# Value product in two portions a tile, early scores in more PSUM banks, sums of one element in an attention and mixer kernel

## The chip, the cores and the metric

The kernel runs on one core of a Trainium2 chip. The metric is the device time of one execution in microseconds (us). A core has five engines that work side by side, each through its own instructions in order: TensorE (PE, matrix products; its weight loads are listed as PEld), VectorE (DVE), ScalarE (ACT), GpSimd (POOL) and SyncE (SP), which here only issues DMA transfers. They meet at semaphores. Matrix products land in PSUM, eight banks of 2 KB per partition; DVE and ACT carry results from there to SBUF.

## The reference

Talking-heads attention, 4 batches (b), 12 heads, 448 positions, 64 elements a head, followed by an MLP mixer, all float32:

```
scores = einsum('bhij,hg->bgij', scale * q @ k.T, w_pre)     # heads mixed before the softmax
e      = exp(scores - max(scores))
attn   = e / (sum(e) + 1e-9)
attn   = einsum('bhij,hg->bgij', attn, w_post)               # heads mixed after it
x      = attn @ v                                            # then (B, 448, 768)
u      = x + (relu(x.T @ w_tok1) @ w_tok2).T
out    = u + relu(u @ w_ch1) @ w_ch2
```

## The kernel before

The first half of the time is attention, the second half the mixer, which the change does not touch.

**Tiles and groups.** The 448 query positions of a batch are cut into tiles of 120, 120, 120 and 88 rows (`IT`), so there are 16 tiles T. For each tile `qk` makes the scores S of all 12 heads, one pair of heads a call: two products into two PSUM banks, then two copies to SBUF. `regroup` rearranges S by DMA on SP: a group G is ten query rows of all 12 heads. A tile of 120 rows has 12 groups, one of 88 rows has 9 (eight of ten rows and one of eight). There are 180 groups. `first[T]` is the first group of tile T.

**Steps.** The groups are taken in steps of two (the last group of an 88-row tile is a step of its own; a group of eight rows goes through smaller matrices, `kpre8`, `kpost8`). For one step `pre` (L210) mixes the heads of both groups into a PSUM tile "pre" of two banks, `mx` (L220, DVE) takes the row maximum, `ex` (L228, ACT) the exponential with its row sum, `rec` (L237, L238 on DVE, L241 on POOL) adds 1e-9 to the sums of both groups in one instruction, takes the reciprocal, and scales the matrix `wr` that mixes the heads afterwards. Then for each group `post` (L253, PE) mixes the heads and transposes into a bank "post", and `hi` (L270, ACT) copies that bank to AT, the attention of the tile. `av` (L278, PE) multiplies one pair of heads of a finished tile with V into one bank "av"; a copy on DVE (L284) and a DMA on SP (L287) follow. The two heads of a pair go to the two halves of the columns of the PE array, `qk` of the later tiles and `post` use all columns.

**Order.** The order of instructions on every engine is that of the program text (a manual schedule). The main loop goes over the steps. In step i it issues the regroupings of later groups, then at the first group `pre` of step i+2, `rec` of step i+1, `mx` and `ex` of step i+2; then for each group `post`, `hi`, the value products due there, the scores due there, and conversions. What is due at which group stands in two tables, `qk_at` and `do`, filled ahead of the loop (L464 to L488): while the groups of tile U are worked on, `qk` makes the scores of tile U+2 and `av` the value product of tile U-1. Before, the six `av` of a tile are spread evenly, one at every second group of a 12-group tile.

**Conversions.** Scores of tiles 2 to 15 use operands split in two parts of a rounded type. `conv_k` (L126 on ACT, then L127 on POOL) and `conv_q` (L153, L154) make them. Tiles 0 and 1 use the raw K and Q (L180), with the copy of S on ACT for the first head of a pair and on DVE for the second; later tiles have both copies on DVE (L186).

**PSUM.** The eight banks are two "pre" tiles of two banks, two "post" banks and two "av" banks. A `qk` takes either both "av" banks or one "pre" tile.

**The start.** WARM products on zeros come first. Then `qk` of tile 0 (pairs in turn in "pre" and "av"), the first regroupings, and part of tile 1's `qk`; the rest of tile 1 comes inside the first two groups.

**The end of attention.** At the last tile's second group the pools for the mixer are opened (`open_prep`) and weight conversions (`cv_tick`) begin to share ACT, DVE and POOL; behind the last group come transposes `tr` and the `av` of tile 15.

Of the kernel before, what the change touches and what calls it, by code (L numbers as in the profile page):

```python
# [8 lines left out]
F32 = mybir.dt.float32  # L9
# [16 lines left out]
HP = H // 2  # L26
# [11 lines left out]
def attn_mixer_kernel(  # L38
# [12 lines left out]
    nc = tc.nc  # L51
# [12 lines left out]
    def en(name, **kw):  # L64
        p = tc.alloc_tile_pool(name=name, reuse_waits="tile", **kw)
        opens[name] = p
        return p
# [5 lines left out]
    ps_av = en("ps_av", bufs=2, space=PSUM)  # L73
# [4 lines left out]
    ps = en("ps", bufs=2, space=PSUM)  # L78
# [15 lines left out]
    for b in range(B):  # L94
        for t in range(4):
            n = IT[t][1]
# [67 lines left out]
            nc.sync.dma_start(out=V[b][p:p + n, :, part, :], in_=v[b, j % 128:j % 128 + n, :, j // 128, :])  # L164
            j += n

    def qk(T, h, split=False):
        b, t = divmod(T, 4)
        n = IT[t][1]
        if T not in S_t:  # L170
            S_t[T] = early.tile([120, H, S], F32, tag="s", name="s")
        if split:
            p2 = ps.tile([128, 2, 512], F32, tag="pre", name="qk")
            p = [p2[:, s] for s in range(2)]
        else:
            p = [ps_av.tile([128, 512], F32, tag="av", name="qk") for s in range(2)]
        for s in range(2):
            if T < 2:
                g, rs = HP * s + h, slice(64 * s, 64 * s + 64)
                nc.tensor.matmul(out=p[s][:n, :S], lhsT=Q[T][rs, h, :], rhs=K0[rs, h, :], start=True, stop=True)  # L180
            else:
                g = 2 * h + s
                kt = K[b, h][:, s, :]
                for i, l in enumerate(Q[T, g // 6]):
                    nc.tensor.matmul(out=p[s][:n, :S], lhsT=l[:, g % 6, :], rhs=kt, start=i == 0, stop=i == 1)  # L185
            (nc.vector.tensor_copy if s or T > 1 else nc.scalar.copy)(out=S_t[T][:n, g, :], in_=p[s][:n, :S])  # L186
# [9 lines left out]
    def regroup(G):  # L196
        b, t, c, n = groups[G]
        o = 4 if n == GR else 0
        nc.sync.dma_start(out=rt[G % NR][o:o + 12 * n], in_=rows(G)(S_t[4 * b + t], 0))

    def pre(st):
        p = ps.tile([128, 2, 512], F32, tag="pre", name="pre")
        PP[st[0]] = p
        if len(st) == 1:
            nc.tensor.matmul(out=p[:96, 0, :S], lhsT=kpre8, rhs=rt[st[0] % NR][:96], start=True, stop=True)
            return
        for x in range(2):
            k = slice(64 * x, 64 + 60 * x)
            for s, a in enumerate(st):
                nc.tensor.matmul(  # L210
                    out=p[64 * s:64 * s + 64, x, :S], lhsT=kpre[k], rhs=rt[a % NR][k], start=True, stop=True
                )

    def parts(G):
        return 128 if groups[G][3] == GR else 96
# [7 lines left out]
    def ex(st):  # L223
        m = parts(st[0])
        s, p = SM[st[0]], PP.pop(st[0])
        for x, G in enumerate(st):
            e = mid.tile([128, S], F32, tag="e", bufs=6, name="e")
            nc.scalar.activation(  # L228
                out=e[:m], in_=p[:m, x, :S], func=ACTF.Exp, bias=s[:m, x:x + 1], scale=1.0,
                accum_out=s[:m, 2 + x:3 + x],  # L230
            )
            E[G] = e

    def rec(st):
        m, w, n = parts(st[0]), len(st), groups[st[0]][3]
        s = SM.pop(st[0])
        nc.vector.tensor_scalar_add(out=s[:m, 4:4 + w], in0=s[:m, 2:2 + w], scalar1=1e-9)  # L237
        nc.vector.reciprocal(out=s[:m, 6:6 + w], in_=s[:m, 4:4 + w])  # L238
        for x, G in enumerate(st):
            r = mid.tile([128, 120], F32, tag="wr", bufs=4, name="wr")  # L240
            nc.gpsimd.tensor_scalar(  # L241
                out=r[:m, :12 * n], in0=kpost if n == GR else kpost8, scalar1=s[:m, 6 + x:7 + x], scalar2=None,
                op0=ALU.mult,
            )
            WR[G] = r
# [10 lines left out]
    def hi(G):  # L256
        b, t, c, n = groups[G]
        T = 4 * b + t
        if T not in AT:
            AT[T] = atp.tile([JP, JT, H, 120], F32, tag="at", bufs=2, name="at")  # L260
        d = AT[T].rearrange("p j g i -> p (j g) i")
        p = PO.pop(G)[:JP, :JT * H * n]
        if n < GR:
            d, p = d[:, :, 10:88:11], p.rearrange("p (q i) -> p q i", i=n)
        else:
            w = 10 if t < 3 else 11
            a = w * (c - c % 2)
            d = d[:, :, a:a + 2 * w].rearrange("p q (s i) -> p q s i", s=2)[:, :, :, 5 * (c % 2):5 * (c % 2) + 5]
            p = p.rearrange("p (q s i) -> p q s i", s=2, i=5)
        nc.scalar.copy(out=d, in_=p)  # L270
# [32 lines left out]
    for i in range(WARM):  # L303
        p = ps.tile([128, 512], F32, tag="post", name="pw")
# [3 lines left out]
    for x in range(2):  # L308
        ps_ = slice(64 * x, 64 * x + 64)
        nc.vector.tensor_tensor(  # L310
            out=kpre[ps_, :60].rearrange("p (i g) -> p i g", i=5),
            in0=kcat[0][ps_, :12].unsqueeze(1).to_broadcast([64, 5, H]),
# [4 lines left out]
        out=kpost.rearrange("p (g i) -> p g i", g=H), in0=kcat[1][:, 12:24].unsqueeze(2).to_broadcast([128, H, GR]),  # L317
# [5 lines left out]
        out=kpre8.rearrange("p (i g) -> p i g", i=8), in0=k8[:, :12].unsqueeze(1).to_broadcast([96, 8, H]),  # L323
# [4 lines left out]
        out=kpost8.rearrange("p (g i) -> p g i", g=H), in0=k8[:, 12:24].unsqueeze(2).to_broadcast([96, H, 8]),  # L328
        in1=k8[:, 24:32].unsqueeze(1).to_broadcast([96, H, 8]), op=ALU.mult,
    )  # L330
    for h in range(HP):
        qk(0, h, h % 2 == 0)
    for G in range(NR):
        regroup(G)
    for h in range(2):
        qk(1, h)
    steps = []
    G = 0
    while G < NG:
        n = 2 if groups[G][2] % 2 == 0 and groups[G][3] == GR else 1  # L340
# [2 lines left out]
    pre(steps[0])  # L343
    mx(steps[0])
    ex(steps[0])
    pre(steps[1])
    qk(1, 2)
    rec(steps[0])
    mx(steps[1])
    ex(steps[1])  # L350
    pre_done = steps[AH][0]
    done_r = NR

# [105 lines left out]
    qk_at, do = {}, {}  # L459

    def at(G, *a):
        do.setdefault(max(0, G), []).append(a)

    for h in range(3):  # L464
        qk_at.setdefault(min(h, 1), []).append((1, 3 + h))
    for i, g in enumerate((0, 0, 1, 1, 2, 4, 5, 6, 7, 8, 9, 10)):
        at(g, conv_k, 0, i)
    for T in range(2, NT):
        f = first[T - 1]
        n = first[T] - f - 4  # L470
        for h in range(HP):
            g = f - 9 + h * n // 5 if T > 2 else (5, 6, 7, 8, 9, 11)[h]
            qk_at.setdefault(g, []).append((T, h))
            if T % 4 == 3 and T + 1 < NT:
                c = [f - 7 + i + (i > 5) + (i > 6) for i in range(H)]
                at(c[2 * (h - KB) + 1] + 1 if h >= KB else f - LR - 2 + h, load_k, T // 4 + 1, h)
                for i in (2 * h, 2 * h + 1):
                    at(c[i], conv_k, T // 4 + 1, i)
        at(max(first[T - 2] - LR + 2, 7 * (T - 2)), load_q, T)
        for hf in range(2):  # L480
            at(f - 13 + 2 * hf if T > 2 else 3 + 3 * hf, conv_q, T, hf)
    for T in range(NT - 1):
        f, n = first[T + 1], first[T + 2] - first[T + 1]
        for hp in range(HP):
            at(f + hp * n // HP, av, T, hp)
    for b in range(B):
        for part in range(JT):
            at(first[4 * b] + 3 + part, load_v, b, part)  # L488
# [1 line left out]
    for i, st in enumerate(steps):  # L490
        while done_r < min(NG, st[0] + LR + 2, pre_done + NR):
            regroup(done_r)
            done_r += 1
        nxt = steps[i + AH] if i + AH < len(steps) else []
        for G in st:
            b, t, c, n = groups[G]
            if (b, t, c) == (B - 1, 3, 1):
                close("early")
                open_prep()
                cv_tick(2)  # L500
                load_x(0)
            for fn, *a in do.get(G, []):
                if fn in (load_k, load_q, load_v):
                    fn(*a)
            if G == st[0]:
                if nxt:
                    pre(nxt)
                    pre_done += len(nxt)
                if i + 1 < len(steps):
                    rec(steps[i + 1])  # L510
                if nxt:
                    mx(nxt)
                    ex(nxt)
            post(G)
            hi(G)
            for fn, *a in do.get(G, []):
                if fn is av:
                    fn(*a)
            for a in qk_at.get(G, []):
                qk(*a)  # L520
            for fn, *a in do.get(G, []):
                if fn in (conv_k, conv_q):
                    fn(*a)
            if (b, t) == (B - 1, 3) and c:
                cv_tick(c % 2)
                if c == 5:
                    load_x(1)
# [190 lines left out]
```

## Time and profile before

| | |
|---|---|
| median of 3 runs | 915.91 us (912.76 to 915.93) |
| the profiled execution, its own time | 916.81 us |
| span of the program in it | 915.0 us |
| mean granted TensorE clock | 0.991 |
| start to the first group's `post` | 0 to 31.15 us |
| tile 0 (12 groups) | 31.15 to 69.95 us |
| tiles 1 to 15 | 69.95 to 468.60 us |
| transposes, `av` of tile 15, mixer | 468.60 to 915.0 us |

The page lists busy times by engine and groups of instructions by line. A row of the timeline gives start and length in us, engine, line, operation, output and inputs, how many instructions were merged into the row, and in brackets how long the engine had been idle before it and what ended that. PE's matrix instructions overlap, their ends are modelled, and a row's length contains a tail; so the time that a row takes from PE is read from its start to the start of the next row, and is called its slot below. Every float32 product shows as two matrix instructions: a `post` is 8 of them, an `av` 16, a `pre` 8, a later `qk` 4.

### The profile page before, as it was taken

The numbers are of one execution on the slowest core, as the hardware profiler recorded it, in microseconds if no ns is written. First come the engines' busy times: TensorE is split into PE (matmuls) and PEld (weight loads), VectorE is DVE, ScalarE is ACT, GpSimd is POOL, SyncE is SP. The second block draws the span as 40 slices with busy tenths as digits, with TensorE's granted clock in tenths as the row PEclk, the third lists the DMA queues.
The fourth block names the chain that finished last, engine by engine and source line by source line (L and its number), as shares of the span: only waits on it lengthen the run. The fifth ranks groups of instructions, "written<-read, shape, count | busy, mean of one in ns | idle before, by whom it ended". The sixth has DMA issues, their size and how long they took to land.

```text
span 915.0 us, 16574 instructions
## 1 busy us (share of the span) xinstructions
PE 890.0 (97%) x6227; PEld 705.9 (77%) x6227; DVE 475.5 (52%) x928; ACT 372.6 (41%) x861; POOL 316.9 (35%) x358
## 2 busy tenths in 40 slices
PE   8869999999999999999979999999999999999998
PEld 3346777767777677777768888999999999999997
DVE  2445665766565765665468999998300120031102
ACT  2565755467555564654555453443100100010000
POOL 3374743347333563332344567775000000000000
PEclk9899999999999999999998999999999999999999
DMA  3564553845437454553464666654500030001001
GB/s 94 181 173 127 160 134 110 198 152 162 134 118 195 153 152 130 145 153 103 104 215 143 197 234 193 172 170 136 192 1 1 1 120 1 1 19 43 1 1 60
DMA packets 82703, 109.31 MB, mean 119 GB/s; under 512 B 40835, under 2 KB 69056, under 8 KB 82112
## 3 DMA queue, kind: packets, MB, share of 16 engines
q1 hardware_dynamic: 82176, 107.34, 39.6%
q10 hardware_dynamic: 320, 0.87, 0.4%
q8 instruction: 49, 0.80, 0.4%
q14 instruction: 30, 0.25, 0.1%
q0 software_dynamic: 128, 0.05, 0.0%
HBM read 53.18 MB, written 16.52 MB: 76 GB/s over the span
## 4 chain that ended last, share of the span: by engine, by line
PE 89%; DVE 4%; ACT 3%; DMA 2%; issue 1%; POOL 1%; SPq 0%; POOLq 0%; ACTq 0%; DVEq 0%
PE post L253 16%; PE av L278 9%; PE qk L185 8%; PE pre L210 8%; PE pc L557 6%; PE pc L556 6%; PE pc L558 6%; PE po L557 6%; PE po L558 6%; PE po L556 6%; PE pt L556 2%; PE pt L557 2%; PE pt L558 2%; PE qk L180 2%; ACT e L228 1%; DVE sm L220 1%
## 5 line engine op out<-in xcount | busy, mean ns | idle before, releaser
L253 PEld LDWEIGHTS post<-wr,e 128*112 128x112 f32 (+1 forms) x1440 | 162.6, 177 | 75.9 <-issue 51.4
L253 PE MATMUL post<-wr,e 128*112 128x120 f32 (+1 forms) x1440 | 188.6, 275 | 2.4 <-ACT at L270 1.8
L228 ACT ACTIVATE e<-pre,sm 128x448 f32<-128x448 f32 x180 | 112.6, 630 | 157.7 <-DVE sm L220 157.7
L241 POOL TENSOR_SCALAR wr<-kpost,sm 128x120 f32<-128x120 f32 x180 | 102.6, 581 | 161.2 <-DVE sm L238 143.9
L553 DVE SCALAR_TENSOR_TENSOR rl<-pc,rh 128x448 fp32r<-128x448 f32 x48 | 29.9, 622 | 222.0 <-ACT rh L552 222.0
L186 DVE COPY s<-qk 120x448 f32<-120x448 f32 (+1 forms) x180 | 105.5, 621 | 68.5 <-PE qk L185 51.8
L552 ACT ACTIVATE rh<-pc 128x448 fp32r<-128x448 f32 x48 | 26.0, 543 | 238.8 <-PE pc L558 238.8
L270 ACT COPY at<-post 112x480 f32<-112x480 f32 x180 | 106.9, 616 | 24.4 <-PE post L253 24.4
L220 DVE TENSOR_REDUCE sm<-pre 128x2 f32<-128x896 f32 (+1 forms) x92 | 98.5, 1070 | 35.0 <-PE pre L210 34.0
L557 PE MATMUL pc<-u,w 128*128 128x448 f32 x288 | 105.2, 365 | 0.0
L556 PE MATMUL pc<-u,w 128*128 128x448 f32 x288 | 105.2, 365 | 0.0
L558 PE MATMUL pc<-u,w 128*128 128x448 f32 x288 | 105.2, 365 | 0.0
L558 PE MATMUL po<-rh,w 128*128 128x448 f32 x288 | 105.2, 365 | 0.0
L556 PE MATMUL po<-rh,w 128*128 128x448 f32 x288 | 105.2, 365 | 0.0
L557 PE MATMUL po<-rl,w 128*128 128x448 f32 x288 | 105.2, 365 | 0.0
L185 PE MATMUL qk<-k,qc 128*120 128x448 f32 (+1 forms) x336 | 95.6, 398 | 7.3 <-POOL k L127 4.4
L278 PE MATMUL av<-at,v 112*64 112x120 f32 (+1 forms) x1536 | 95.5, 267 | 3.7 <-DVE x L284 3.7
L412 POOL TENSOR_SCALAR cv_g<-cv_g 128x384 f32<-128x384 f32 (+2 forms) x56 | 86.8, 1550 | 21.9 <-ACT cv_g L406 21.9
L210 PE MATMUL pre<-r,kpre 64*64 64x448 f32 (+1 forms) x704 | 89.9, 576 | 0.7 <-issue 0.4
L278 PEld LDWEIGHTS av<-at,v 112*64 112x64 f32 x1536 | 74.9, 138 | 15.3 <-DVE x L284 4.4
L284 DVE COPY x<-av 128x120 f32<-128x120 f32 (+1 forms) x96 | 34.6, 360 | 70.3 <-PE av L278 69.3
L185 PEld LDWEIGHTS qk<-k,qc 128*120 128x120 f32 (+1 forms) x336 | 49.2, 174 | 27.8 <-DVE x L284 9.4
(81 smaller groups left out, 1127.8 us busy)
## 6 DMA issues: line engine op xcount, KB each, us to landing
r<-s SPq DMA_DIRECT2D x176, 210.0 KB
cv_r<-in_w_ch_dram SPq DMA_DIRECT2D x48, 384.0 KB
rq<-in_q_dram SPq DMA_DIRECT2D x40, 180.0 KB
xr<-x_dr SPq DMA_DIRECT2D x8, 672.0 KB
u_dr<-u SPq DMA_DIRECT2D x24, 224.0 KB
ur<-u_dr SPq DMA_DIRECT2D x4, 1344.0 KB
out_dram<-ur SPq DMA_DIRECT2D x24, 224.0 KB
x_dr<-x SPq DMA_DIRECT2D x72, 60.0 KB
```

Of the source, the lines that this page charges most:

```text
L185: nc.tensor.matmul(out=p[s][:n, :S], lhsT=l[:, g % 6, :], rhs=kt, start=i == 0, stop=i == 1)
L186: (nc.vector.tensor_copy if s or T > 1 else nc.scalar.copy)(out=S_t[T][:n, g, :], in_=p[s][:n, :S])
L210: nc.tensor.matmul(out=p[64 * s:64 * s + 64, x, :S], lhsT=kpre[k], rhs=rt[a % NR][k], start=True, stop=True)
L220: nc.vector.tensor_reduce(out=s[:m, 0:w], in_=PP[st[0]][:m, :w, :S], axis=AX.X, op=ALU.max, negate=True)
L228: nc.scalar.activation(out=e[:m], in_=p[:m, x, :S], func=ACTF.Exp, bias=s[:m, x:x + 1], scale=1.0, accum_out=s[:m, 2 + x:3 + x],)
L241: nc.gpsimd.tensor_scalar(out=r[:m, :12 * n], in0=kpost if n == GR else kpost8, scalar1=s[:m, 6 + x:7 + x], scalar2=None, op0=ALU.mult,)
L253: nc.tensor.matmul(out=p[:JP, j * m:(j + 1) * m], lhsT=l, rhs=w[:k, :m], start=True, stop=True)
L270: nc.scalar.copy(out=d, in_=p)
L278: nc.tensor.matmul(out=p[64 * s:64 * s + 64, :n], lhsT=V[b][:, 2 * hp + s, j, :], rhs=AT[T][:, j, 2 * hp + s, :n], start=j == 0, stop=j == ...
L556: nc.tensor.matmul(out=p, lhsT=a[0], rhs=x[0], start=first, stop=False)
L557: nc.tensor.matmul(out=p, lhsT=a[0], rhs=x[1], start=False, stop=False)
L558: nc.tensor.matmul(out=p, lhsT=a[1], rhs=x[0], start=False, stop=last)
```

## The change

Five things, all in the attention half.

1. `av` of a tile is issued three pairs at a time, at two groups: offsets 1 and 9 in a tile of 12 groups, 7 and 8 in one of 9.
2. Within a group the scores due there are issued ahead of the value products, where they came behind them.
3. Tile 0's and tile 1's scores use banks of all three kinds: `qk` takes the name of a home. Three pairs of tile 1 are made ahead of the first regrouped data, the other three between the first two steps' `pre` and `ex`, none inside the main loop.
4. The conversions of batch 0's K and of tile 2's Q, and tile 2's scores, move by a group or two.
5. `rec` adds 1e-9 to each group's sum in an instruction of its own.

```diff
-    def qk(T, h, split=False):
+    def qk(T, h, home="av"):
...
-        if split:
+        if home == "pre":
             p2 = ps.tile([128, 2, 512], F32, tag="pre", name="qk")
             p = [p2[:, s] for s in range(2)]
         else:
-            p = [ps_av.tile([128, 512], F32, tag="av", name="qk") for s in range(2)]
+            pool = ps_av if home == "av" else ps
+            p = [pool.tile([128, 512], F32, tag=home, name="qk") for s in range(2)]
...
-        nc.vector.tensor_scalar_add(out=s[:m, 4:4 + w], in0=s[:m, 2:2 + w], scalar1=1e-9)
+        for x in range(w):
+            nc.vector.tensor_scalar_add(out=s[:m, 4 + x:5 + x], in0=s[:m, 2 + x:3 + x], scalar1=1e-9)
...
     for h in range(HP):
-        qk(0, h, h % 2 == 0)
+        qk(0, h, ("pre", "av", "pre", "post", "pre", "av")[h])
     for G in range(NR):
         regroup(G)
-    for h in range(2):
-        qk(1, h)
+    for h in range(3):
+        qk(1, h, ("post", "av", "post")[h])
...
     ex(steps[0])
+    qk(1, 3)
     pre(steps[1])
-    qk(1, 2)
+    qk(1, 4)
     rec(steps[0])
     mx(steps[1])
     ex(steps[1])
+    qk(1, 5)
...
-    for h in range(3):
-        qk_at.setdefault(min(h, 1), []).append((1, 3 + h))
-    for i, g in enumerate((0, 0, 1, 1, 2, 4, 5, 6, 7, 8, 9, 10)):
+    for i, g in enumerate((0, 0, 1, 3, 3, 4, 6, 7, 8, 8, 9, 10)):
         at(g, conv_k, 0, i)
...
-            g = f - 9 + h * n // 5 if T > 2 else (5, 6, 7, 8, 9, 11)[h]
+            g = f - 9 + h * n // 5 if T > 2 else 6 + h
...
-            at(f - 13 + 2 * hf if T > 2 else 3 + 3 * hf, conv_q, T, hf)
+            at(f - 13 + 2 * hf if T > 2 else 2 + 3 * hf, conv_q, T, hf)
     for T in range(NT - 1):
         f, n = first[T + 1], first[T + 2] - first[T + 1]
         for hp in range(HP):
-            at(f + hp * n // HP, av, T, hp)
+            at(f + ((7, 8) if n < 12 else (1, 9))[hp // 3], av, T, hp)
...
             post(G)
             hi(G)
+            for a in qk_at.get(G, []):
+                qk(*a)
             for fn, *a in do.get(G, []):
                 if fn is av:
                     fn(*a)
-            for a in qk_at.get(G, []):
-                qk(*a)
```

## The prediction

> **What bounds the kernel now.** I read the page's first part, then the busy times of stretches, then the timeline of PE, then single waits.
>
> ```profile
> PE 890.0 (97%) x6227; PEld 705.9 (77%) x6227; DVE 475.5 (52%) x928; ACT 372.6 (41%) x861; POOL 316.9 (35%) x358
> ...
> 24.30:31.20 6.90, 6.14 (x29) 1.88 (x29) 3.22 (x6) 1.76 (x5) 0.70 (x2) 0.75 0.65 245
> 31.20:70.00 38.80, 28.99 (x181) 16.63 (x181) 17.71 (x36) 25.03 (x58) 25.86 (x29) 0.94 0.58 156
> ...
> 209.40:238.20 28.80, 28.80 (x269) 20.47 (x265) 18.34 (x38) 19.37 (x47) 19.79 (x22) 1.00 0.55 141
> ...
> 428.20:451.60 23.40, 23.40 (x244) 16.76 (x240) 11.03 (x26) 13.98 (x36) 7.41 (x13) 1.00 0.48 113
> ```
>
> The columns are the stretch, its length, the busy time of PE, PEld, DVE, ACT, POOL, the granted clock, DMA. From 209.4 (tile 6) and 428.2 (tile 14) on PE is busy all the time; the other engines have a third or more free. In tile 0 (31.2 to 70.0) PE lacks 9.8 us. So two things can be gained: PE's own time per tile, and the holes of tile 0.
>
> Being busy hides what a change of matrix shape costs. The timeline of PE in tiles 5 to 7 and at the end of attention:
>
> ```profile
> 203.80 0.98 PE L210 MATMUL pre<-r,kpre 64*64 64x448 f32 x8
> ...
> 208.50 0.98 PE L210 MATMUL pre<-r,kpre 64*64 64x448 f32 x8
> ...
> 217.10 0.98 PE L210 MATMUL pre<-r,kpre 64*64 64x448 f32 x8
> 218.01 1.07 PE L253 MATMUL post<-wr,e 128*112 128x120 f32 x8
> 219.02 1.04 PE L278 MATMUL av<-at,v 112*64 112x120 f32 x16
> 219.99 1.22 PE L185 MATMUL qk<-k,qc 128*120 128x448 f32 x4
> 221.05 0.98 PE L253 MATMUL post<-wr,e 128*112 128x120 f32 x8
> 221.79 1.05 PE L185 MATMUL qk<-k,qc 128*120 128x448 f32 x4
> 222.78 0.98 PE L210 MATMUL pre<-r,kpre 64*64 64x448 f32 x8
> ...
> 245.13 1.89 PE L253 MATMUL post<-wr,e 128*112 128x120 f32 x16
> 246.95 1.04 PE L278 MATMUL av<-at,v 112*64 112x120 f32 x16
> ...
> 472.64 1.43 PE L278 MATMUL av<-at,v 112*64 112x88 f32 x32
> 474.62 0.83 PE L278 MATMUL av<-at,v 112*64 112x88 f32 x16 [0.54 <-DVE x L284]
> 476.10 0.83 PE L278 MATMUL av<-at,v 112*64 112x88 f32 x16 [0.65 <-DVE x L284]
> 477.84 0.99 PE L278 MATMUL av<-at,v 112*64 112x88 f32 x16 [0.91 <-DVE x L284]
> ```
>
> Slots, start to start: pre 0.91, post between pre and av 1.01, av 0.97. But two posts in a row take 1.82, so the second adds 0.81. An av in a row: two of 88 columns last 1.43 and one 0.83, so the second adds 0.60; by columns (120/88) that is 0.82 for 120. A lone av thus pays 0.15 in its own slot and 0.19 in the post that it parts from the next: 1.82 for two posts becomes 1.01 + 0.97 + 1.00.
>
> The other limit is a chain. `hi` of a step waits on ACT behind `ex` of two steps on, and the next step's post waits for the bank that `hi` frees:
>
> ```profile
> 179.50 0.98 PE L210 MATMUL pre<-r,kpre 64*64 64x448 f32 x8
> 180.26 1.32 POOL L154 TENSOR_TENSOR qc<-rq,qc 128x528 fp32r<-128x528 f32 x1 [2.49 <-ACT qc L153]
> 180.28 1.33 DVE L237 TENSOR_SCALAR sm<-sm 128x2 f32<-128x2 f32 x1
> 181.72 1.09 DVE L220 TENSOR_REDUCE sm<-pre 128x2 f32<-128x896 f32 x1
> 184.88 1.04 PE L253 MATMUL post<-wr,e 128*112 128x120 f32 x8 [0.50 <-ACT at L270]
> ...
> 431.23 0.98 PE L210 MATMUL pre<-r,kpre 64*64 64x448 f32 x8
> 432.38 1.09 DVE L220 TENSOR_REDUCE sm<-pre 128x2 f32<-128x896 f32 x1 [0.96 <-PE pre L210]
> 433.15 1.04 PE L278 MATMUL av<-at,v 112*64 112x120 f32 x16
> 434.24 0.37 DVE L284 COPY x<-av 128x120 f32<-128x120 f32 x1 [0.77 <-PE av L278]
> 435.12 0.98 PE L210 MATMUL pre<-r,kpre 64*64 64x448 f32 x8
> ```
>
> Undisturbed, `mx` starts 1.15 behind its pre (431.23, 432.38). At 184.88, where the chain did end last, the post came 3.16 behind `mx` (181.72). So the next step's first post can't come before 4.31 behind a pre, and as it stands 0.91 behind its own pre, **no step can be shorter than 3.40** after a step without stall. The step with one av lasts 3.89 (431.23 to 435.12) and never feels this.
>
> **The change part by part.** The sum is against the profiled execution, 916.81 us; the median of the runs shown, 915.91, lies 0.90 below it.
>
> Portions, steady part. A lone av costs 3.89 minus a bare step (0.91 + 1.82 = 2.73), so 1.16, and six 6.96 a tile. A portion stands between the step's last post and the next pre: the first av 0.97, the other two 0.82 each, 2.61; two portions 5.22. That saves 1.74. For 88 columns each av is shorter by the same on both sides, so the saving holds.
>
> Scores ahead of av. A qk at the end of a step adds 0.81 (203.80 to 208.50 is 4.70, minus 3.89). One right behind an av adds 0.98 (217.10 to 222.78 is 5.68, minus 4.70), 0.17 more. In the old tables two qk of a 12-group tile stand so (three in the third tile of a batch), and five in a 9-group tile: about three on average, 0.5 a tile. None does after.
>
> What is added. In three of four tiles one portion shares its group with a qk (offsets 9, 9, 8), which holds both "av" banks:
>
> ```profile
> 216.12 1.06 PE L185 MATMUL qk<-k,qc 128*120 128x448 f32 x4
> ...
> 216.80 1.16 DVE L186 COPY s<-qk 120x448 f32<-120x448 f32 x2 [1.03 <-PE qk L185]
> ```
>
> The first of the two copies ends 0.68 + 0.58 behind the qk's start, 0.07 on for the release: 1.33, where the qk's slot on PE is 0.98. The first av waits 0.35 there, 0.26 a tile on average. Behind it stand the other two av and the next pre; that is in the sum. Within a portion the third av needs the bank of the first: copied 1.09 behind its start in 0.37 (433.15, 434.24), free at about 1.55, and the third is due at 1.64. It fits by 0.1, if DVE is idle; I take 0.1 of loss a portion for these seams, bounds none and 0.70 for each av after the first (the mean of the waits at 474.62, 476.10 and 477.84).
>
> The chain. A step with one qk lasts 3.54 (2.73 + 0.81) against 3.40: not bound, but only just. A bare step lasts 2.73 and is held at 3.40, 0.67 lost. Bare steps come once in the third tile of a batch (0.17 a tile on average) and four times in tile 14, which makes no scores: 1.74 gained, 2.68 lost, so tile 14 gets slower by 0.9. Tile 15 has bare steps too; I take nothing for it.
>
> So a steady tile gains 1.74 + 0.5 - 0.26 - 0.17 = 1.81. Tiles 1 to 13: 23.5. Less 0.9 for tile 14, less 3.0 for 30 portions' seams: **19.6**.
>
> Sums of one element:
>
> ```profile
> L237 DVE TENSOR_SCALAR sm<-sm 128x2 f32<-128x2 f32 x88 | 23.0, 262 | 12.3 <-ACT e L228 11.8
> ...
> L237 DVE TENSOR_SCALAR sm<-sm 96x1 f32<-96x1 f32 x4 | 0.6, 141 | 0.0
> ```
>
> It adds 88 instructions of some 0.14 to DVE, which has a third free; half of that lies in waits for ACT. The mean of 262 holds a few long ones: the one at 180.28 ends when POOL's L154 does (180.26 + 1.32). Whether one element waits for POOL as well no row shows; the four of 96x1 last 0.14. I take it that they don't, which returns the 0.5 of 184.88; bounds: 0.5 gained and, if they do wait, 6 lost (below). The Trainium skill bears on this: VectorE: DVE Perf Modes, section What auto-detection actually checks, lets such an instruction with one source in SBUF read through two ports if its outermost non-unit dimensions are even or equal in source and destination, and SBUF — State Buffer, section Who interferes with whom, has it then wait for GpSimd as a whole. For two elements the trace agrees (1.33 against POOL's 1.32). For one element the wording "or equal" would leave the wait in place, and the sum would be 0.5 less.
>
> Opening. Up to tile 0's regroupings nothing moves: its scores and their copies keep their order. Tile 1's last three pairs come ahead of the loop. That puts two S copies on DVE ahead of the first `rec` (up to 2 us later), but PE no longer stalls for them between the first groups. In tile 0:
>
> ```profile
> 48.38 0.88 PE L185 MATMUL qk<-k,qc 128*120 128x448 f32 x3 [1.23 <-POOL qc L154]
> ...
> 57.53 0.88 PE L185 MATMUL qk<-k,qc 128*120 128x448 f32 x3 [1.68 <-POOL qc L154]
> ...
> 61.21 0.67 PE L185 MATMUL qk<-k,qc 128*120 128x448 f32 x2 [1.57 <-POOL k L127]
> ...
> 67.87 0.67 PE L185 MATMUL qk<-k,qc 128*120 128x448 f32 x2 [2.85 <-POOL k L127]
> ...
> 69.95 1.94 PE L253 MATMUL post<-wr,e 128*112 128x120 f32 x8
> ```
>
> 7.3 us of waits for conversions, each with its qk one group behind the conversion. After the change a qk stands two groups behind, all but the last. POOL's 25.86 and ACT's 25.03 of work in these 38.8 us stay, and they feed each other, so the stage can't fall below some 29 (PE's 28.99); the bounds are -2 and 9.8. I take half: **5**. Conversions and loads moved past each other on POOL and SP have their data long before in the steady part. Of SP's work, three stores of x now wait in a row ahead of the regroupings, by up to a portion (2.6), while those run four steps ahead.
>
> Sum: 19.6 + 0.5 + 5 = 25.1; and 1 for tile 1's start: behind the hole at 67.87 its first post lasted 1.94 (69.95) where others last 1.07. 916.8 - 26.1 = 890.7, by the median 889.8: **890**.
>
> **The rivals.**
> *The two banks hold the portion back* (the slower one). From 474.62 on each av behind others waited for DVE, 0.70 on average. If every second and third av of a portion waits so, 60 x 0.70 = 42 is lost: 890 + 42 - 3 (already counted) = 929. Slower from 0.5 per av on. For it: only 0.1 of slack. Against: there DVE had conversions to do, here it is idle at offsets 1, 7, 8 and 9 but for S copies. Half of it, the third av alone at 0.3, gives 896.
> *The chain is later than I think.* The slack is 0.14 in some 30 one-qk steps (nine a batch): 0.2 us more from pre to `mx` costs 0.06 x 30 = 2, 0.4 costs 8. For it: S copies of a qk at a step's end (216.80 to 217.96, beyond the pre at 217.10) and then two sums stand ahead of `mx`. Against: `mx` was still on time there but for the wait on POOL. With waits for POOL kept (some ten steps of 0.6): 896. Together 895 to 904.
> *The opening doesn't do what it says*: ACT and POOL keep each other waiting, nothing gained: 895; with the later `rec`, 897.
> *The clock.* PEclk 0.75 over 24.30 to 31.20 is 3.45 us at half clock, 1.7 lost, behind a stretch with waits. Were each portion's wait to bring one such window, 30 x 1.7 = 51: 941. Against: in tile 0, with holes of 1.2 to 2.9 us, the clock was 0.94 all the same. The Trainium skill, TensorE: Matmul & The Clock Gate, section A second HAM failure mode: psum-queue depth-cycling, describes this: cycling through PSUM banks leaves short idle gaps that re-throttle the clock. The trace speaks against it for 0.35 us.
>
> **How the numbers follow.** Forecast 890 (884 to 895) 0.55; chain or banks partly (895 to 908) 0.26, of it 0.08 by sums that still wait for POOL; opening without gain 0.10; banks in full 0.04, clock 0.02; several of these at once, within 0.5% (911.3 to 920.5), 0.03. 0.5% is about what a measurement here can tell from no change. Faster 0.91, same 0.03, slower 0.06. The range 882 to 903 holds the forecast, the opening and more than half of the second case.
>
> **What would show it.** Rows of three av in a row with 0.82 from start to start and no DVE wait behind them; two portions a tile; steady tiles of 12 groups near 27 us (tile 6: 28.8); tile 14 longer than 23.4; ACT `hi` as what ends the holes of PE in bare steps only; no L237 beyond 0.2 us; tile 0 near 34 us. Wrong would be: waits of av for DVE in most portions, holes before post in one-qk steps, or tile 0 as long as before.

## The result and the profile after

The changed kernel takes 887.5 us (median of 4 runs, 886.28 to 888.43), the one before 915.16 (4 runs); the ratio is 0.9701, interval 0.9678 to 0.9725. The forecast was 890 with a range of 882 to 903. The profiled execution of the changed kernel has a span of 885.3 us against 915.0.

Lines move by one to four: sums L239, post L255, `hi` L272, av L280, its copy L286, later qk L186. The page's first part and one stretch, which holds tile 0 (32.99 to 62.58) but for its last 0.6 us:

```profile
PE 855.2 (97%) x6227; PEld 701.1 (79%) x6227; DVE 467.4 (53%) x1016; ACT 368.5 (42%) x861; POOL 317.2 (36%) x358
```

```profile
31.00:62.00 31.00, 23.52 (x174) 15.77 (x178) 17.36 (x42) 23.87 (x56) 25.74 (x29) 1.00 0.81 205
```

PE is as full as before with as many instructions, and it is busy for 34.8 us less (890.0 to 855.2): the time came out of "busy". Where, by stage (from the first post of a tile to that of the next; the mixer counts from its first transpose):

| stage | before | after | gained | forecast |
|---|---|---|---|---|
| start to tile 0 | 31.15 | 32.99 | -1.84 | 5.0, both together |
| tile 0 | 38.80 | 29.59 | 9.21 | |
| tiles 1 to 13 | 358.30 | 337.06 | 21.24 | 22.0 |
| tile 14 | 23.35 | 23.53 | -0.18 | -0.9 |
| tile 15 | 16.99 | 15.97 | 1.02 | 0 |
| mixer | 446.40 | 446.12 | 0.28 | 0 |
| sum (parts rounded) | 915.0 | 885.3 | 29.7 | 26.1 |

The timeline of PE in tile 5, a step with a portion and one in which the portion stands behind a qk:

```profile
166.02 1.90 PE L255 MATMUL post<-wr,e 128*112 128x120 f32 x16
167.85 2.68 PE L280 MATMUL av<-at,v 112*64 112x120 f32 x48
170.46 0.98 PE L211 MATMUL pre<-r,kpre 64*64 64x448 f32 x8
...
184.48 1.05 PE L186 MATMUL qk<-k,qc 128*88 128x448 f32 x4
185.84 2.68 PE L280 MATMUL av<-at,v 112*64 112x120 f32 x48 [0.31 <-DVE s L187]
188.45 0.98 PE L211 MATMUL pre<-r,kpre 64*64 64x448 f32 x8
```

Three av show as one row of 48, from 167.85 to the pre at 170.46: 2.61 us, as worked out. There is no hole inside. Behind a qk the portion waits: the qk's slot is 1.36 (184.48 to 185.84) instead of 0.98, 0.38 lost where 0.35 was forecast.

Tile 14, which makes no scores and so has bare steps:

```profile
404.99 1.89 PE L255 MATMUL post<-wr,e 128*112 128x120 f32 x16
406.81 0.98 PE L211 MATMUL pre<-r,kpre 64*64 64x448 f32 x8
408.38 1.86 PE L255 MATMUL post<-wr,e 128*112 128x120 f32 x16 [0.58 <-ACT at L272]
410.18 0.98 PE L211 MATMUL pre<-r,kpre 64*64 64x448 f32 x8
411.49 1.86 PE L255 MATMUL post<-wr,e 128*112 128x120 f32 x16 [0.33 <-ACT at L272]
```

This is the ACT chain: post waits for the copy `hi` of the step before. From pre to pre the step takes 3.37 (406.81 to 410.18), by the forecast 3.40; the next takes 3.10 (to the pre at 413.28), less than the limit that the prediction took for general. Outside tile 14 the same wait of 0.58 stands once per third tile of a batch, on the first post of the next tile.

The sums, from the list of groups by shape and from the view of their line (shortest, median and longest in ns):

```profile
L239 DVE TENSOR_SCALAR sm<-sm 128x1 f32<-128x1 f32 x176 | 19.6, 147 | 18.6 <-ACT e L229 18.2
```

```profile
L239 DVE TENSOR_SCALAR sm<-sm x180: 138/145/160, 31.0 to 430.6; 128x1 f32<-128x1 f32 x176, 96x1 f32<-96x1 f32 x4
```

No sum takes longer than 160 ns, where two elements took up to 1329. Twice as many instructions use 19.6 us in place of 23.0.

Tile 0, the waits of 0.4 us or more that are left on PE:

```profile
37.15 1.04 PE L255 MATMUL post<-wr,e 128*112 128x120 f32 x8 [1.35 <-ACT at L272]
...
41.63 1.89 PE L255 MATMUL post<-wr,e 128*112 128x120 f32 x16 [1.13 <-POOL wr L243]
...
46.88 1.07 PE L255 MATMUL post<-wr,e 128*112 128x120 f32 x8 [2.44 <-POOL wr L243]
...
57.50 0.66 PE L186 MATMUL qk<-k,qc 128*120 128x448 f32 x2 [0.40 <-POOL k L127]
...
61.06 0.67 PE L186 MATMUL qk<-k,qc 128*120 128x448 f32 x2 [1.67 <-POOL k L127]
```

The waits of qk for conversions went from 7.3 us to 2.1. In their place post waits 3.6 us for `wr`, which POOL makes behind the conversions; POOL is busy 25.7 of these 31 us and ends 5.6 of the 7.3 us of holes that PE has left in tile 0. So the holes shrank only from 9.8 to 7.3 us. The larger part of the 9.2 us gained is work: PE is busy 22.25 us in tile 0 (stretch 32.99 to 62.58) where it was 28.99. Scores of tile 1 moved ahead of the stage, and two stretches at a granted clock of 0.50 in the execution before (38.0 to 41.5, and from 68.8 on) have no counterpart in this one.

### The profile page after: what moved, and what is told of

It is laid out like the page before. It is cut to its first block, busy times and chain, and to the rows that moved or that the text cites. A ratio compares the mean times of both kernels' runs of the same rounds, so it can differ in the third digit from the quotient of the medians.

```text
span 885.3 us, 16665 instructions
## 1 busy us (share of the span) xinstructions
PE 855.2 (97%) x6227; PEld 701.1 (79%) x6227; DVE 467.4 (53%) x1016; ACT 368.5 (42%) x861; POOL 317.2 (36%) x358
## 4 chain that ended last, share of the span: by engine, by line
PE 87%; DVE 5%; DMA 3%; ACT 2%; POOL 2%; issue 1%; SPq 0%; DVEq 0%; POOLq 0%; ACTq 0%
PE post L255 15%; PE av L280 9%; PE pre L211 8%; PE qk L186 7%; PE pc L560 7%; PE pc L559 7%; PE pc L558 7%; PE po L560 6%; PE po L559 6%; PE po L558 6%; PE pt L558 2%; DMA r<-s 2%; PE pt L559 2%; PE pt L560 2%; PE qk L181 1%
## 5 line engine op out<-in xcount | busy, mean ns | idle before, releaser
L255 PEld LDWEIGHTS post<-wr,e 128*112 128x112 f32 (+1 forms) x1440 | 158.7, 177 | 75.5 <-issue 57.1
L255 PE MATMUL post<-wr,e 128*112 128x120 f32 (+1 forms) x1440 | 176.3, 271 | 9.5 <-ACT at L272 5.7
L272 ACT COPY at<-post 112x480 f32<-112x480 f32 x180 | 104.6, 617 | 4.3 <-PE post L255 4.1
L186 PE MATMUL qk<-k,qc 128*120 128x448 f32 (+1 forms) x336 | 89.2, 386 | 2.5 <-POOL k L127 2.1
L280 PE MATMUL av<-at,v 112*64 112x120 f32 (+1 forms) x1536 | 82.2, 263 | 7.0 <-DVE x L286 3.8
L211 PE MATMUL pre<-r,kpre 64*64 64x448 f32 x704 | 87.4, 561 | 0.6 <-DMA r<-s 0.6
L280 PEld LDWEIGHTS av<-at,v 112*64 112x64 f32 x1536 | 74.7, 138 | 14.1 <-DVE s L187 7.1
L286 DVE COPY x<-av 128x120 f32<-128x120 f32 (+1 forms) x96 | 34.5, 360 | 59.1 <-PE av L280 53.1
L154 POOL TENSOR_TENSOR qc<-rq,qc 128x720 fp32r<-128x720 f32 (+1 forms) x28 | 45.2, 1613 | 50.2 <-ACT qc L153 49.6
```

The lines of the kernel that those rows point to most:

```text
L211: nc.tensor.matmul(out=p[64 * s:64 * s + 64, x, :S], lhsT=kpre[k], rhs=rt[a % NR][k], start=True, stop=True)
L255: nc.tensor.matmul(out=p[:JP, j * m:(j + 1) * m], lhsT=l, rhs=w[:k, :m], start=True, stop=True)
L280: nc.tensor.matmul(out=p[64 * s:64 * s + 64, :n], lhsT=V[b][:, 2 * hp + s, j, :], rhs=AT[T][:, j, 2 * hp + s, :n], start=j == 0, stop=j == ...
```

## The experiments

The theory: a lone av between two posts costs 1.16 us of PE, a portion of three at a step's end 2.61, and that is the steady gain; the opening gains on its own. The rivals are named with each run. A warning for all totals: the executions differ by more than the small effects, in two places that don't depend on the edit. The opening runs through stretches of half clock (e8_warm), and in three of the twelve profiled ones the products of the mixer take 2% longer, so that the mixer lasts 453 us in place of 446 (last section). I therefore read small effects from the stages. From tile 2 on they agree within about 0.1 us a tile. Tile 1 does not: in nine of the twelve profiled executions, the one before among them, a stretch at half clock falls into it and makes it 0.8 to 1.9 us longer than the second tiles of later batches. The changed kernel's two and e9's have none there, so 1.0 of the 21.24 us gained in tiles 1 to 13 belongs to the clock.

### e1_spread: portions undone

```diff
-            at(f + ((7, 8) if n < 12 else (1, 9))[hp // 3], av, T, hp)
+            at(f + hp * n // HP, av, T, hp)
...
             hi(G)
-            for a in qk_at.get(G, []):
-                qk(*a)
             for fn, *a in do.get(G, []):
                 if fn is av:
                     fn(*a)
+            for a in qk_at.get(G, []):
+                qk(*a)
```

> Value products spread one by one over the even groups and ahead of the scores again, the rest as changed. Theory (what a lone av costs between two posts is the steady gain): tiles 1 to 13 go back to 28.5, 28.75, 24.9 and 27.3 us, 21 us more together, tile 15 about 1 more, the opening stays at 62.6: 908 to 910 us. Rival (the single sums or the opening carry the steady tiles): they stay near 27 us and the whole under 895.

Measured: 910.6 us, before on the same chip 916.49, ratio 0.9942 (0.9908 to 0.9976). Tiles 4 to 7 take 27.32, 28.48, 28.73 and 24.87, tiles 1 to 13 together 357.81, as before (358.30). Its timeline of PE in tile 5:

```profile
172.16 1.07 PE L255 MATMUL post<-wr,e 128*112 128x120 f32 x8
173.16 1.04 PE L280 MATMUL av<-at,v 112*64 112x120 f32 x16
174.13 1.07 PE L255 MATMUL post<-wr,e 128*112 128x120 f32 x8
175.14 0.98 PE L211 MATMUL pre<-r,kpre 64*64 64x448 f32 x8
```

The old slots are back: 1.00, 0.97, 1.01. So the steady gain is that of the portions with the order; the opening carries none of it, and the sums 0.5 us in one tile: tile 5 takes 28.48 where it took 29.00 before, which held the wait of 0.50 at 184.88. What is left against the kernel before, 5.9 us between the medians (2.2 to 8.4 by the interval), comes from the opening, with the clock in it, and from tile 15 (0.7).

### e2_order: scores behind the portion again

```diff
             hi(G)
-            for a in qk_at.get(G, []):
-                qk(*a)
             for fn, *a in do.get(G, []):
                 if fn is av:
                     fn(*a)
+            for a in qk_at.get(G, []):
+                qk(*a)
```

> Portions kept, but the scores of a group behind its portion, as before. Theory: in the ten groups that have both, the portion no longer waits 0.31 for the banks, but the qk behind an av costs 0.16 more and waits about 0.1 for the last copy: within 1.5 us of the changed kernel, 886 to 889. Rival (the order is what makes the portions cheap): 0.4 or more in each of ten groups and late S copies ahead of mx, 892 or more.

Measured: 888.26 us, ratio to the kernel before 0.9698 (0.9653 to 0.9742). The step of tile 5 in which both stand:

```profile
183.81 2.68 PE L280 MATMUL av<-at,v 112*64 112x120 f32 x48
186.42 0.98 PE L186 MATMUL qk<-k,qc 128*88 128x448 f32 x3
```

No wait for banks ahead of the av, and the tile takes 26.84 in place of 26.89; tiles 4, 7 and 8 are 0.09, 0.20 and 0.10 shorter. So the change of order gains nothing; it loses about 0.1 us in a tile that has both in one group. What the prediction booked under this heading, the dear qk behind an av, went away because portions share a group with a qk only ten times, where single av did 38 times.

### e3_sums: one sum of two elements again

```diff
-        for x in range(w):
-            nc.vector.tensor_scalar_add(out=s[:m, 4 + x:5 + x], in0=s[:m, 2 + x:3 + x], scalar1=1e-9)
+        nc.vector.tensor_scalar_add(out=s[:m, 4:4 + w], in0=s[:m, 2:2 + w], scalar1=1e-9)
```

> One sum of two elements per step again, the rest as changed. Theory (a two-element sum waits for POOL, a one-element sum does not, and the chain now has little slack): some ten sums of 0.7 to 1.3 us, each putting off mx and so the next step's first post by up to 0.6: 2 to 6 us more, 889 to 894. Rival (the waits lie in slack): 887.5, within 1 us.

Measured: 889.96 us, ratio 0.9737 (0.9682 to 0.9793). The third tiles of a batch take 27.52 in place of 27.16, second tiles up to 0.05 more, others the same (tile 1, with its half clock, left aside): 1.2 us in all. The view of the sums' line, then the timeline of all engines at one of them:

```profile
L238 DVE TENSOR_SCALAR sm<-sm x92: 140/159/969, 27.9 to 430.5; 128x2 f32<-128x2 f32 x88, 96x1 f32<-96x1 f32 x4
```

```profile
101.27 2.24 POOL L127 TENSOR_TENSOR k<-rk,k 64x448 fp32r<-64x448 f32 x2
...
101.47 0.95 DVE L238 TENSOR_SCALAR sm<-sm 128x2 f32<-128x2 f32 x1
...
102.54 1.09 DVE L221 TENSOR_REDUCE sm<-pre 128x2 f32<-128x896 f32 x1
...
103.55 1.15 DVE L187 COPY s<-qk 120x448 f32<-120x448 f32 x2
...
104.21 1.26 PE L186 MATMUL qk<-k,qc 128*120 128x448 f32 x4
```

The sum lasts 0.95, to the end of POOL's first conversion (101.27 and half of 2.24). It is one of twenty that take 0.66 to 0.97 us here, and every one of them ends 0.02 to 0.03 behind the end of a conversion on POOL. In the changed kernel 50 of the 180 one-element sums lie wholly inside a running instruction of POOL, and none takes longer than 0.16. The rest follows in DVE's order: `mx` ends late, the S copies start late, and a second qk in the step holds its bank for longer: its slot is 1.20 (to the pre at 105.41) in place of 0.98. So the wait is real and the cure works, for 1.2 us; not by the ACT chain, as I had said, but by the copies behind `mx`, and in one step a batch only. The totals don't separate the two kernels.

### e4_opening and e5_sched: the opening undone, whole and in part

e4 puts back all of the opening; e5 only its times, which the diff shows:

```diff
-    for i, g in enumerate((0, 0, 1, 3, 3, 4, 6, 7, 8, 8, 9, 10)):
+    for i, g in enumerate((0, 0, 1, 1, 2, 4, 5, 6, 7, 8, 9, 10)):
...
-            g = f - 9 + h * n // 5 if T > 2 else 6 + h
+            g = f - 9 + h * n // 5 if T > 2 else (5, 6, 7, 8, 9, 11)[h]
...
-            at(f - 13 + 2 * hf if T > 2 else 2 + 3 * hf, conv_q, T, hf)
+            at(f - 13 + 2 * hf if T > 2 else 3 + 3 * hf, conv_q, T, hf)
```

> Opening as before (homes, tile 1's scores inside the first groups, old times of the first conversions and of tile 2's scores), the rest as changed. Theory (the opening gains by itself): tile 1's first post at 69 to 70 us instead of 62.6, the steady tiles as changed: 893.5 to 896. Rival (the opening is shorter for the portions, the sums or the phase of the clock): 62.6 to 66 and under 891.

> Homes and tile 1's scores as changed, but the old times of batch 0's and tile 2's conversions and of tile 2's scores. Theory (tile 0 gains by scores standing two groups behind their conversions): tile 0 goes from 29.6 to 31.4 back to 35 or more, with PE waiting for POOL before qk. Rival (it gains by tile 1's scores having left the first groups): tile 0 stays at 30 to 32.

Measured: e4 896.29 us (889.93 to 901.77), ratio 0.9793 (0.9725 to 0.9861); e5 891.13, ratio 0.9716 (0.9669 to 0.9764). In e4 tile 1's first post came at 64.17, not at 69 to 70, which is what the rival had said; but the profiled execution had its first regrouping at 16.42, five us ahead of the kernel before and the changed one, by the clock. Counted from the first regrouping to tile 1's first post the runs can be compared, as far as the clock lets them:

| | first regrouping | tile 0's first post | tile 1's first post | from first to last |
|---|---|---|---|---|
| before | 21.31 | 31.15 | 69.95 | 48.64 |
| e4 (old opening) | 16.42 | 25.97 | 64.17 | 47.75 |
| e5 (old times alone) | 19.97 | 31.53 | 66.19 | 46.22 |
| changed | 21.43 | 32.99 | 62.58 | 41.15 |

Within these stretches the clock was at 0.50 for 8.0 us in the kernel before, 6.3 in e4, 1.9 in e5 and 0.7 in the changed kernel, and the same stretch lasts 41.15 to 43.40 in the nine profiled executions that have the new opening. So the old opening costs 4.4 to 6.6 us more than the new, and its times alone 2.8 to 5.1. The 1.5 between e4 and e5 lies within what the clock can do; a gain by the homes is not shown. The homes with tile 1's scores bring tile 0's first post 2 us later (11.56 behind the first regrouping against 9.55), and tile 0 takes 3.5 less (38.20 to 34.66), at most 2.2 of it by the clock. e5's waits in the timeline of PE:

```profile
44.85 0.88 PE L186 MATMUL qk<-k,qc 128*120 128x448 f32 x3 [1.50 <-POOL qc L154]
...
53.56 0.88 PE L186 MATMUL qk<-k,qc 128*120 128x448 f32 x3 [1.34 <-POOL qc L154]
...
57.23 0.66 PE L186 MATMUL qk<-k,qc 128*120 128x448 f32 x2 [1.57 <-POOL k L127]
...
63.89 0.67 PE L186 MATMUL qk<-k,qc 128*120 128x448 f32 x2 [2.85 <-POOL k L127]
```

They are the four waits of before, within 0.4 us each and 7.3 in all, on the same queue: the times of the qk and of their conversions are what made them.

### e6_moved: portions where nothing else is due

```diff
-            at(f + ((7, 8) if n < 12 else (1, 9))[hp // 3], av, T, hp)
+            at(f + (hp * 2 + 1 if T == 13 else ((7, 8) if T == 14 else (5, 7) if n < 12 else (1, 11) if T % 4 == 1 else (1, 5))[hp // 3]), av, T, hp)
```

> The changed kernel with the portions put where no scores are due and where the step was bare: offsets 1 and 5 in the first two tiles of a batch, 1 and 11 in the third, 5 and 7 in the 9-group tiles, tile 14 one av at each odd offset; tile 15 as changed. Theory (a portion behind a qk waits 0.38 for the banks, a bare step loses 0.6 to the ACT chain): tiles of the first two kinds 26.5 and 25.3, the third 26.5, 9-group tiles 23.2, tile 14 about 22.3 instead of 23.5; 6 to 7 us less in tiles 1 to 14. Rival (those waits are made up by PE or come back elsewhere): within 1.5 us of the changed kernel's stages.

Measured: 882.26 us (6 runs, 876.88 to 888.68), ratio 0.9637 (0.9582 to 0.9693). Tiles 4 to 7 take 25.39, 26.51, 26.70 and 22.75, tile 14 22.25; tiles 1 to 14 353.96 in place of 360.59. That is 6.6 less, in the places that were named (7.4 less without tile 1, which has half clock here). Between 60 and 419 us no hole of 0.1 or more is left on PE. Tile 14:

```profile
395.56 1.04 PE L280 MATMUL av<-at,v 112*64 112x120 f32 x16
396.53 0.98 PE L211 MATMUL pre<-r,kpre 64*64 64x448 f32 x8
397.44 1.89 PE L255 MATMUL post<-wr,e 128*112 128x120 f32 x16
399.27 1.04 PE L280 MATMUL av<-at,v 112*64 112x120 f32 x16
```

A lone av at a step's end takes 0.97, and the step 3.71 (395.56 to 399.27) where it took 3.89 with the av between its posts. So part of the gain is the place and part the row: of the 1.74 us saved by six av, place alone gives 6 x 0.19 = 1.1, being in a row the rest.

### e7_six: all six in one portion

```diff
-            at(f + ((7, 8) if n < 12 else (1, 9))[hp // 3], av, T, hp)
+            at(f + (hp * 2 + 1 if T == 13 else (7, 8)[hp // 3] if T == 14 else 11 if T % 4 == 1 else 5), av, T, hp)
```

> As e6_moved, but all six pairs in one portion (offset 5, in the third tile of a batch 11; tiles 14 and 15 as there). Theory (each av in a row costs 0.82, the run of them only 0.15 at its ends, two banks are enough at any length): a portion of six 5.07 us without waits for DVE, 0.15 less than two of three; but the step at offsets 0 and 1 becomes bare and loses 0.6 to the chain: tiles of 12 groups 0.4 longer than in e6_moved, 9-group tiles 0.15 shorter. Rival (the copies on DVE fall behind in a longer run): waits of av for DVE from the third on, 1 us or more a tile.

Measured: 890.58 us, ratio 0.9711 (0.9655 to 0.9768). The timeline in tile 4, the long portion (88 columns) and a new hole:

```profile
140.54 1.89 PE L255 MATMUL post<-wr,e 128*112 128x120 f32 x16 [0.94 <-POOL wr L243]
...
146.72 3.94 PE L280 MATMUL av<-at,v 112*64 112x88 f32 x96
150.58 0.98 PE L211 MATMUL pre<-r,kpre 64*64 64x448 f32 x8
```

Six av take 3.86 without a hole; two banks are enough for six. With 120 columns the step at offset 5 lasts 2.46 longer than with three, 0.82 for each, and 9-group tiles are 0.15 shorter, as worked out. 12-group tiles got longer: 0.5 in the second tile of a batch, as the chain says (a hole of 0.59), but 0.9 in the first and 1.6 in the third, where post waits for `wr`, which POOL makes behind conversions. I had not seen that one: here a short step behind a conversion is bound by POOL as well.

### e8_warm: no hole ahead of the first scores

```diff
-WARM = 11
+WARM = 18
```

> 18 products on zeros at the start instead of 11, so that PE has no hole before the first scores; the rest as changed. Theory (the time of the opening differs between executions by windows of half clock, which a hole ahead of the first scores brings): no half clock between 8 and 22 us, first regrouping at 16 to 18 us, up to 4 us less than the changed kernel's profiled execution. Rival (the half clock comes from the scores themselves, which leave PE holes of 0.6): first regrouping anywhere from 16 to 21.5, as without.

Measured: 885.76 us, ratio 0.9668 (0.9615 to 0.972). Busy times by stretch of the changed kernel, then of this one, in its profiled execution:

```profile
8.50:22.00 13.50, 11.56 (x31) 4.41 (x32) 4.42 (x9) 3.72 (x7) 0.81 (x2) 0.50 0.18 39
...
600.00:850.00 250.00, 250.00 (x1235) 231.68 (x1235) 47.89 (x85) 29.39 (x57) 2.39 (x2) 1.00 0.11 39
```

```profile
8.50:22.00 13.50, 10.25 (x45) 3.79 (x46) 6.34 (x13) 4.79 (x9) 0.81 (x2) 1.00 0.35 105
...
600.00:850.00 250.00, 250.00 (x1211) 227.04 (x1210) 46.61 (x81) 28.54 (x56) 1.66 (x1) 1.00 0.11 39
```

In the same stretch PE has 45 matrix instructions instead of 31, at a granted clock of 1.00 instead of 0.50. The first regrouping comes at 16.74 instead of 21.43, the mixer starts 3.1 us earlier (436.07, 439.14); part of the rest went to a stretch of half clock from 57.4 to 60.8. In the profiled executions with 11 products the first regrouping came at 16.00 to 21.43, so 16.74 alone speaks against neither side. What speaks against the rival is that the scores leave the same holes of 0.62 to 0.66 us here (ahead of 9.38, 11.80 and 14.23) and the clock stays at 1.00 all the same.

### e9_best and e10_after: the two together, and the change beside them

> e6_moved and e8_warm together. Theory (both gains are stages of their own): first regrouping at 16 to 17.5 us, tiles 1 to 14 as in e6_moved (353 to 354 us), 8 to 10 us less than the changed kernel run beside it where the mixer runs equally fast. Rival (the half clock only moves to a later window): no gain over e6_moved, 6 to 7 us less than the changed kernel.

> The changed kernel itself, beside e9_best on the same chip: 884 to 892 us, tiles 1 to 14 at 360 to 361 us; the opening between the extremes of the other runs by the windows of half clock.

Measured: e9 877.19 us (6 runs, 876.69 to 878.18), ratio to the kernel before 0.9595 (0.9572 to 0.9618); the changed kernel on the same chip 888.53 (five runs of 883.41 to 888.70, one of 897.27), ratio 0.9706 (0.9678 to 0.9734). First regrouping at 16.38 and 17.47, tiles 1 to 14 352.79 and 360.49. 11 us between the medians, 6 between the profiled spans (875.7, 881.6), whose opening and mixer ran alike within 2. That 6 is the rival's number and not the 8 to 10 of the theory. The profiled execution of the changed kernel was the fastest of its six and left the warm products little to gain; a stretch of half clock stands in e9's tile 0 (42.9 to 46.3), as the rival had it; and tile 15 is 1.4 longer in e9 (17.37, 15.99): one post waits 1.39 for `hi` there, which was not traced further. That the warm products do gain is seen in the medians, of whose 11.3 us tiles 1 to 14 explain 7.7, and in the mean granted clock, 0.994 in all six runs of e9 and at most 0.992 in those of the changed kernel. e9 beats both kernels and varies least.

## Why the prediction was right

**A lone av costs 1.16, a portion 2.61.** Right in the tiles of 12 groups, seen in the rows of after and, undone, in e1: there the terms without seams add up to 1.6 to 1.7 us a tile, and 1.6 were gained. In the tiles of 9 groups the price doesn't hold. Three of their six av stood at a step's end already (offsets 1, 3 and 7; the one at 246.95 is in the prediction's own lines, behind two posts in a row), where e6 shows 0.97 and not 1.16; that is 0.6 too much. By the terms (1.74 + 5 x 0.17 - 0.35) these tiles would gain 2.2 each, and they gained 1.2 to 1.35; the other 0.4 was not traced. So some 3 us of the steady sum were not there, and the 3.0 booked for seams, which were not there either, made up for them. That the sum came out at 21.24 against 22.0 is partly luck. The price came from comparing slots of one instruction with different neighbours, which a view of busy time can't show. The Trainium skill (TensorEngine Tiling (Array Packing), section Key Properties) says that a change of tiling mode drains the engine, which is in accord with this; the runs show the 0.15 and 0.19 of the seams, not what they consist of.

**Scores ahead of av, 0.5 a tile.** In the tiles of 12 groups the term fits, but its cause was misnamed: e2 shows that the order gives nothing.

**Bank wait 0.35, chain 3.40.** 0.38 and 3.37 in the trace; e6 removes both and gains 6.6, of 6 to 7 worked out for it. The chain was taken too hard in a run of bare steps (3.10 for the second), so tile 14 lost 0.2 instead of 0.9.

**Seams within portions, 3.0 in all.** Mis-sized: nothing was lost, with three av or six.

**One-element sums, 0.5.** Right that they don't wait, and right in size: tile 5 in e1. With two elements in the changed kernel the loss is 1.2 us, not 6, by another way than the chain.

**Opening 5.** The term was mis-sized: 7.4 between the profiled executions, of which e4 puts 4.4 to 6.6 on the change; the rest lies with the clock. Half of the mechanism was right: qk waits 2.1 us for its conversions instead of 7.3 (undone in e5), and tile 0's first post comes later. The other half was missing. The prediction took PE's 28.99 us of work in tile 0 as a floor and half of the 9.8 us of holes as the gain; the work fell to 22.25, and the holes only to 7.3.

**Tile 1's start, 1.** The 1.0 was gained, by luck. The first post of 1.94 at 69.95 stood in a stretch at a granted clock of 0.50 (68.8 to 72.2). The change doesn't keep that away: e2 to e8 have half clock in the same tile.

**Tile 15**, taken as nothing, gained 1.0. e1, with av spread, has 16.25 there, so the portions give 0.3; the rest was not traced to a cause.

The rivals: no av waited for a bank inside a portion, only its first one behind a qk (0.31 to 0.40, ten times); and the clock didn't fall in steady tiles (1.00 in all profiled runs from tile 2 to the mixer).

## What to carry to other kernels

Where an engine is busy all the time, read what one instruction takes by its neighbours, from start to start. Grouping matmuls of one shape, and putting the odd one at a step's end, shortened PE's busy time here without taking away a single instruction. Price each place by its own neighbours: a price from one kind of tile was wrong for another. Before groups are made, list what each step keeps: a step that gets too short falls to the next chain (ACT here, POOL in e7), and a group that meets another user of its banks waits. Timed differences below 1% want stages read from traces, and the granted clock of each stage beside them, when the start of the kernel depends on the clock.

## What the runs showed of the hardware

Half clock in the opening comes in pieces of 3.4 us and multiples of it (the stretches between changes of the granted clock in the traces). In nine profiled executions with 11 warm products the clock is on record ahead of the first scores. Seven of them fell to 0.50 between 8 and 10 us, behind holes of 0.9 to 1.9 us ahead of the first scores; two, with holes of 0.7 and 1.1, didn't before 20 us. A hole of 1.9 us was followed by 13.7 us at 0.50 in the changed kernel; with the hole filled the clock stayed at 1.00 to 57 us in e8 and to 43 us in e9. That the hole is the cause rests on these counts; the execution with 1.1 shows that its length alone doesn't decide.

The profile of the kernel before has no record of the clock ahead of 20.98 us and counts that as 1.00. But eight matrix instructions of the first scores take 3.35 us there (from 9.23), as in the changed kernel at 0.50 (3.35 from 9.34), against 1.77 in e8 (from 9.38). So its opening ran slowly too, and its mean clock of 0.991 is too high.

In three profiled executions (e2, e7, e8) the products of the mixer take 2% longer at a granted clock of 1.00: 1211 against 1235 matrix instructions in 250 us above. The program of the mixer is the same in all twelve kernels; the cause stays open.

A two-element sum on DVE waits for a POOL instruction to end, a one-element sum doesn't: 969 and 160 ns at most in kernels that differ in nothing else. The Trainium skill (SBUF — State Buffer, section Who interferes with whom) says that a DVE instruction in a mode with two ports and a GpSimd instruction shut each other out for a whole instruction, and names `tensor_scalar` among those that can enter such a mode. The two-element sums agree with that; which mode they ran in no trace shows.
